# Turning two token blocks through one two-bank PSUM tile, and the tail of the first attention ahead of weight conversions

## The chip, the cores and the metric

The kernel runs on one core of one Trainium2 chip. The metric is the device time of one execution in microseconds (us). Each kernel was run several times beside runs of the kernel before on the same chip; medians are quoted with the lowest and the highest run. All runs and all profiles used here have the state fast. A profile comes from one execution, which need not be the median one. Its span is some 2 us shorter than the device time (531.5 us for 533.2).

## The reference

A gated linear attention for 4 batches, 8 heads, 768 tokens and head size 48, followed by a token mixer of rank 32 and a two-layer channel mixer of 384 to 1536 to 384, all in fp32:

```python
for t in range(S):
    state = f[:, :, t, :, None] * state + np.einsum('bhd,bhe->bhde', k[:, :, t], v[:, :, t])
    y[:, :, t] = np.einsum('bhd,bhde->bhe', q[:, :, t], state)
...
xt = x.transpose(0, 2, 1)
h = xt @ U @ V
u = x + h.transpose(0, 2, 1)
ch = np.maximum(u @ w_ch1, 0.0) @ w_ch2
return (u + ch).astype(np.float32)
```

The weights arrive as 64-bit floats and are converted on the chip.

## The kernel before

A batch is four attention units of two heads each. The attention of batch b is interleaved with the mixer of batch b-1, except for the first batch, which has nothing to be interleaved with. There TensorE has gaps, and the author fills some with dummy products of the identity (`busy`) that are meant to keep its clock up. A unit forms, in this order for TensorE, the turned gates, keys (kz) and queries (qT), the sums that enter the state (ds), and the scores (sc); then its output y in two halves, the read of the state and the product of the masked scores (A) with v. A marker copy on ScalarE (seen) stands between the two halves. One weight is converted by two instructions on ScalarE, three on VectorE and one on GpSimd, through a tile `w_y` of which there are two.

```python
def turn(t):                                   # Mixer; one block of 128 tokens
    a = t // 2
    if t % 2 == 0:
        uT[a] = three.tile([P, NDC, 2 * P], F32, name="uT")
    pt = ps_mm.tile([P, 512], F32, name="put", tag="mm")        # one bank, two such buffers
    for m in range(NDC):
        nc.tensor.transpose(pt[:, m * P : (m + 1) * P], x[:, t, m * P : (m + 1) * P], ident)
    if t % 2:
        busy(pt, 2)                            # dummies into the same bank, first batch only
    o = (t % 2) * P
    nc.scalar.copy(uT[a][:, :, o : o + P], pt[:, 0 : NDC * P].rearrange("p (m t) -> p m t", t=P))
# ... cut
# the first batch: tail of the attention, then the mixer
busy(2)
for piece in loads[: early + 1] + rear(HP - 1, "read") + [lambda: busy(2)] + rear(HP - 1, "inner"):
    piece()                                    # loads[i]: one weight's conversion; early is 3
busy(3)
loads = loads[early + 1 :]
m = mixer(0)
start = m.before[:5] + m.firsts[0:1] + m.before[5:7] + m.firsts[1:2] + m.before[7:9]
for i, (_, piece) in enumerate(start + m.firsts[2:]):
    if loads and (i == 0 or i > 4):
        loads.pop(0)()
    piece()
```

`m.before` holds the low-rank product, the sum over groups, the mix (products and the additions to x), then the turns. `m.firsts` holds the first-layer products (names pz and L201 in the profile), each of 128 x 512 outputs for two blocks. ps_mm has two one-bank buffers; ps_big has three two-bank buffers, used for attention and for the mix.

## Time and profile before

| | before |
|---|---|
| median of the runs quoted with the change | 533.25 us (532.75 to 533.78) |
| span of the profile | 531.5 us |
| TensorE busy | 95% |
| granted clock, mean | 0.977 |

The profile has two records of TensorE (and two weight loads) for one fp32 product, and one for a transpose. The granted clock is TensorE's clock as the profile records it, 1.00 for full and 0.50 for half. A row of the costliest groups gives line, engine, operation, output and inputs with their shapes, count, busy time and mean of one, then the engine's idle time just before and what ended it. A row of the list of waits gives who waited for whom, the total, how often, and the longest. First a row of the page, then two rows of the waits of the kernel before from 44 to 90 us:

```profile
L201 PE MATMUL pz<-uT,w 128*128 128x256 f32 x864 | 196.1, 385 | 4.1 <-ACT uT L193 4.1
```

```profile
ACT h L154 <- PE ph L143: 3.4, 1, 3.4
...
PE pz L201 <- ACT uT L193: 3.7, 3, 1.5
```

The first-layer products waited 4.1 us in all for copies of uT, 3.7 of it in the first batch. The copy of h on ScalarE was released by L143, a dummy, and not by the product that it copies.

### The profile page before, as it was taken

To read this page: it belongs to the slowest core of one execution; us is meant where nothing else is said; L and a number is where in the kernel's file an instruction comes from. 1 tells how busy PE (TensorE), PEld (TensorE's weight loads), DVE (VectorE), ACT (ScalarE), POOL (GpSimd) and SP (SyncE) were. 2 spreads that over 40 slices of the span, in tenths; PEclk is the share of its full clock that TensorE was granted. 3 is DMA by queue.
4 is the path that set the end of the run, shared out by engine and by line. 5 is a ranking of instruction groups with operands and counts; after the bars stand their busy time and mean duration, and the time that the engine had idled before them with its cause. 6 is when DMAs were issued, how large, how long until landed. Compare 5 with 4: busy or idle time off the path is not lost.

```text
span 531.5 us, 12234 instructions
## 1 busy us (share of the span) xinstructions
PE 502.3 (95%) x5405; PEld 422.4 (79%) x5405; DVE 269.5 (51%) x396; ACT 146.8 (28%) x297; POOL 30.1 (6%) x49
## 2 busy tenths in 40 slices
PE   6897879999989889999999999999999999999995
PEld 6786558886677546889889877889889878998995
DVE  5885365554678966665666634544222340222232
ACT  2433265551234223232322303321220122102010
POOL 3001134330000000000000000000000000000000
PEclk9996889999999899999999999999999999999998
DMA  9989905423367842241623500010000000000001
GB/s 148 155 214 187 188 19 172 156 71 81 84 96 113 114 85 38 38 59 19 115 29 62 81 5 29 1 23 31 3 2 30 1 31 1 1 30 1 15 17 35
DMA packets 149269, 34.32 MB, mean 65 GB/s; under 512 B 139798, under 2 KB 147670, under 8 KB 149206
## 3 DMA queue, kind: packets, MB, share of 16 engines
q1 hardware_dynamic: 149206, 33.44, 33.0%
q8 instruction: 44, 0.72, 0.6%
q14 instruction: 19, 0.16, 0.1%
HBM read 28.70 MB, written 4.72 MB: 63 GB/s over the span
## 4 chain that ended last, share of the span: by engine, by line
PE 84%; DVE 7%; ACT 4%; issue 2%; DMA 1%; SPq 1%; POOL 1%; DVEq 0%; ACTq 0%; POOLq 0%
PE pz L201 36%; PE pw L246 24%; PE po L223 6%; PE y L664 3%; PE pt L514 2%; PE y L682 2%; PE sc L597 2%; PE ds L634 2%; PE idle L756 2%; DVE Y L566 2%; PE pt L618 2%; DVE X L548 1%; DVE st L649 1%; PE pu L177 1%; PE put L189 1%
## 5 line engine op out<-in xcount | busy, mean ns | idle before, releaser
L201 PE MATMUL pz<-uT,w 128*128 128x256 f32 x864 | 196.1, 385 | 4.1 <-ACT uT L193 4.1
L201 PEld LDWEIGHTS pz<-uT,w 128*128 128x128 f32 x864 | 162.9, 191 | 28.0 <-ACT uT L193 4.0
L208 ACT ACTIVATE z<-pz 128x512 f32<-128x512 f32 x63 | 37.6, 597 | 144.6 <-PE pz L201 140.5
L246 PE MATMUL pw<-w,z 128*128 128x192 f32 x324 | 56.5, 329 | 0.4 <-DVE o L167 0.4
L246 PE MATMUL pw<-zw,w_raw 128*128 128x192 f32 x324 | 55.9, 327 | 0.0
L246 PEld LDWEIGHTS pw<-w,z 128*128 128x128 f32 x324 | 52.8, 190 | 2.3 <-DVE o L167 1.6
L246 PEld LDWEIGHTS pw<-zw,w_raw 128*128 128x128 f32 x324 | 53.0, 190 | 1.3 <-DVE o L167 1.2
L167 DVE TENSOR_TENSOR w_raw<-z 128x768 f32<-128x768 f32 x18 | 17.2, 955 | 55.3 <-ACT z L208 55.3
L548 DVE TENSOR_TENSOR_SCAN X<-fz,ends 128x768 f32<-128x768 f32 x16 | 28.1, 1757 | 18.2 <-ACT fz L535 15.0
L566 DVE TENSOR_TENSOR_SCAN Y<-fz,starts 128x768 f32<-128x768 f32 x16 | 27.9, 1746 | 0.2
L223 PE MATMUL po<-w,zw 128*128 128x384 f32 x72 | 27.0, 519 | 0.5 <-issue 0.5
L604 DVE TENSOR_TENSOR A<-sc,causal 128x768 f32<-128x768 f32 x16 | 15.2, 950 | 23.1 <-PE sc L597 23.1
L68 POOL TENSOR_TENSOR w<-w_y,w_r 128x384 int32<-128x384 int32 x24 | 24.0, 999 | 46.0 <-DVE w_y L67 46.0
L223 PE MATMUL po<-w,z 128*128 128x384 f32 x72 | 25.1, 493 | 1.2 <-DVE o L167 1.2
L649 DVE TENSOR_TENSOR_SCAN st<-added,whole 128x576 f32<-128x576 f32 x16 | 21.7, 1355 | 6.8 <-ACT added L640 6.7
L167 DVE TENSOR_TENSOR w_y<-x,pw 128x192 f32<-128x192 f32 x9 | 3.2, 355 | 38.9 <-ACT w_y L259 38.9
L622 ACT COPY kb<-pt 128x768 f32<-128x768 f32 x16 | 12.8, 798 | 35.7 <-PE pt L618 35.7
L65 DVE TENSOR_SCALAR w_y<-w_y 128x384 f32<-128x384 f32 (+3 forms) x27 | 9.7, 361 | 25.4 <-ACT w_y L63 25.4
L664 PE MATMUL y<-st,qT 48*64 48x48 f32 x704 | 20.3, 265 | 1.5 <-issue 1.5
L664 PEld LDWEIGHTS y<-st,qT 48*64 48x64 f32 x704 | 17.1, 151 | 5.6 <-issue 4.9
L223 PEld LDWEIGHTS po<-w,zw 128*128 128x128 f32 x72 | 13.5, 198 | 9.7 <-issue 2.8
L223 PEld LDWEIGHTS po<-w,z 128*128 128x128 f32 x72 | 13.0, 190 | 9.5 <-DVE o L167 1.8
(105 smaller groups left out, 529.0 us busy)
## 6 DMA issues: line engine op xcount, KB each, us to landing
w_raw<-in_moe_w_ch_dram SPq DMA_DIRECT2D x18, 384.0 KB, 3.1
out_dram<-o SPq DMA_DIRECT2D x24, 192.0 KB, 2.0
f_raw<-in_f_logit_dram SPq DMA_DIRECT2D x16, 144.0 KB, 3.4
k_raw<-in_k_dram SPq DMA_DIRECT2D x16, 144.0 KB, 4.0
q_raw<-in_q_dram SPq DMA_DIRECT2D x16, 144.0 KB, 4.1
v_nat<-in_v_dram SPq DMA_DIRECT2D x16, 144.0 KB, 4.2
v_nat<-in_v_dram SPq DMA_DIRECT2D x32, 72.0 KB, 3.0
zw<-in_moe_w_ch_dram SPq DMA_DIRECT2D x6, 384.0 KB, 7.2
```

The lines of the kernel that those rows point to most:

```text
L68: nc.gpsimd.tensor_tensor(dst.bitcast(I32), shaped(y.bitcast(I32)), shaped(r), ALU.add)
L167: nc.vector.tensor_tensor(*args)
L201: nc.tensor.matmul(pm[:, i * 2 * P : (i + 1) * 2 * P], lhsT=w1[:, m, o : o + P], rhs=uT[a][:, m, :], start=(m == 0), stop=(m == NDC - 1))
L208: nc.scalar.activation(z[a, c][:, k : k + 2, :].rearrange("p i t -> p (i t)"), pm, AF.Relu)
L223: nc.tensor.matmul(pm, lhsT=z[a, i // NI][:, i % NI, s * P : (s + 1) * P], rhs=w2[:, i, :], start=(i == 0), stop=(i == NFC - 1))
L246: nc.tensor.matmul(pm[:, n * HM : (n + 1) * HM], lhsT=lhs[:, i, :], rhs=rhs[:, i, :], start=(i == 0), stop=(i == NI - 1))
L548: nc.vector.tensor_tensor_scan(backwards(X, S - 1, S), backwards(f, S, S), backwards(ends, S - 1, S), 0.0, ALU.mult, ALU.add,)
L566: nc.vector.tensor_tensor_scan(Y, f[:, 0:S], starts, 0.0, ALU.mult, ALU.add)
L604: nc.vector.tensor_tensor(T["A"], sc[:, :, 0 : NBL * C].rearrange("p h (c i) -> p h c i", i=C), causal.unsqueeze(1).unsqueeze(1).broadcast ...
L622: nc.scalar.copy(kb.rearrange("p h c d -> p h (c d)"), pt[:, :, 0 : NBL * PAD])
L649: nc.vector.tensor_tensor_scan(st, added[:, 0 : D * NCH], T["whole"].rearrange("p e c -> p (e c)"), 0.0, ALU.add, ALU.mult)
L664: nc.tensor.matmul(o(c % 2, par, c // 2), lhsT=T["q"][rows[par], chunk[c]], rhs=T["st"][rows[par], c, :], start=(c <= 2), stop=False, skip ...
```

## The change

Its intent: take TensorE's waits and dummies out of the 40 us between the first attention and the steady first-layer products, and free the turns of all batches from the pace of ScalarE. Two blocks are turned into the two banks of one ps_big tile and copied by one instruction; in the first batch, four blocks are turned ahead of the first product and the last two right after it; the dummies write to a bank of their own; on ScalarE the end of the last attention unit goes ahead of all conversions but two. In the opening, kz (keys) goes ahead of the state scan on VectorE, and two dummies go.

```diff
-        def busy(pm, n):
-            for _ in range(n if wide else 0):
-                nc.tensor.matmul(pm[:, DM : DM + P], lhsT=ident, rhs=ident, start=True, stop=True)
...
-            busy(pm, 2)            # low_rank and added_up: ahead of the copies of h
...
-            if t == NCH - 1:
-                busy(pu[0][:, 1], 3)
...
-        def turn(t):
+        def turn(a):
+            uT[a] = three.tile([P, NDC, 2 * P], F32, name="uT")
+            pt = ps_big.tile([P, 2, 512], F32, name="put", tag="big")
+            for s in range(2):
+                for m in range(NDC):
+                    nc.tensor.transpose(pt[:, s, m * P : (m + 1) * P], x[:, 2 * a + s, m * P : (m + 1) * P], ident)
+            nc.scalar.copy(
+                uT[a].rearrange("p m (s t) -> p s m t", s=2),
+                pt[:, :, 0 : NDC * P].rearrange("p s (m t) -> p s m t", t=P),
+            )
...
-        busy(8)
+        busy(6)
...
-            pieces = front(n, "keep") + rear(n - 1, "scan") + front(n, "keys") + rear(n - 1, "scores")
+            pieces = front(n, "keep", "keys") + rear(n - 1, "scan", "scores")
...
-        busy(2)
-        for piece in loads[: early + 1] + rear(HP - 1, "read") + [lambda: busy(2)] + rear(HP - 1, "inner"):
+        for piece in loads[:2] + rear(HP - 1, "read", "inner") + loads[2 : early + 2]:
             piece()
-        busy(3)
-        loads = loads[early + 1 :]
+        loads = loads[early + 2 :]
...
-        start = m.before[:5] + m.firsts[0:1] + m.before[5:7] + m.firsts[1:2] + m.before[7:9]
-        for i, (_, piece) in enumerate(start + m.firsts[2:]):
-            if loads and (i == 0 or i > 4):
-                loads.pop(0)()
-            piece()
+        start = m.before[:5] + m.firsts[0:1] + m.before[5:]
+        idles = {0: 3, 1: 2, 2: 2}
+        for i, (_, piece) in enumerate(start + m.firsts[1:]):
+            busy(idles.get(i, 0))
+            piece()
+            if loads and i not in (1, 2):
+                loads.pop(0)()
```

## The prediction

> **What bounds the kernel now.** I read the page first: busy shares and the chain that ended last.
>
> ```profile
> PE 502.3 (95%) x5405; PEld 422.4 (79%) x5405; DVE 269.5 (51%) x396; ACT 146.8 (28%) x297; POOL 30.1 (6%) x49
> ...
> PE 84%; DVE 7%; ACT 4%; issue 2%; DMA 1%; SPq 1%; POOL 1%; DVEq 0%; ACTq 0%; POOLq 0%
> ```
>
> TensorE is the bound almost everywhere. From 120 us to the end, the list of waits gives it under 7 us of waiting in 410 us. So the change can gain only where TensorE waits, runs dummy products, or runs slowly. The 40 slices show two dips of its clock (6 and 8 tenths), near 50 and 70 us. I therefore read the chain of waits from 38 to 82 us:
>
> ```profile
> 40.26 1.54 issue
> ...
> 50.49 0.44 ACT w_r L64
> 50.93 0.05 ACT seen L671
> 51.02 1.53 PE y L682 x48
> 52.55 1.58 PE idle L756 x6
> 54.13 2.71 PE ph L150 x12
> 56.84 0.73 PE ph L143 x4
> 57.58 0.49 ACT h L154
> ```
>
> Columns are start, length, and what. The last attention unit's second half (L682) waits for the marker copy "seen" on ScalarE, which stands behind conversions of weights. The copy of h, in turn, waits 0.73 us for dummy products L143. Next, the timeline of 60 to 80 us:
>
> ```profile
> 64.37 2.83 PE L201 MATMUL pz<-uT,w 128*128 128x256 f32 x12 [0.66 <-ACT uT L193]
> ...
> 69.88 0.48 ACT L193 COPY uT<-put 128x384 f32<-128x384 f32 x1
> ...
> 70.41 4.54 PE L201 MATMUL pz<-uT,w 128*128 128x256 f32 x12 [1.53 <-ACT uT L193]
> ...
> 78.15 9.12 PE L201 MATMUL pz<-uT,w 128*128 128x256 f32 x41 [1.52 <-ACT uT L193]
> ```
>
> A first product is 12 records. In the steady stretch they come every 216 ns (162 in 35.13 us, from 84.73), so one product takes 2.59 us. Here the first three take from 64.37 to 78.15 + 2.59 = 80.74: 16.4 us in place of 7.8. Between them TensorE turns two blocks and waits for ScalarE, where the copies of uT stand behind conversions. The second also takes 4.54 us. The busy time and granted clock of each microsecond say why (window, length, busy time of TensorE, its weight loads, VectorE, ScalarE and GpSimd, then granted clock, DMA share, GB/s):
>
> ```profile
> 43.00:44.00 1.00, 0.86 (x36) 0.86 (x39) 0.00 (x0) 0.09 (x1) 0.00 (x0) 0.64 0.79 164
> 44.00:45.00 1.00, 1.00 (x48) 1.00 (x45) 0.00 (x0) 0.35 (x1) 0.00 (x0) 0.50 0.67 120
> ...
> 56.00:57.00 1.00, 1.00 (x5) 0.24 (x2) 0.00 (x0) 0.00 (x0) 0.23 (x1) 0.53 0.93 129
> 57.00:58.00 1.00, 0.55 (x4) 0.35 (x4) 0.00 (x0) 0.42 (x1) 0.00 (x0) 1.00 0.73 200
> ...
> 69.00:70.00 1.00, 0.00 (x0) 0.00 (x0) 0.93 (x4) 1.00 (x4) 0.20 (x1) 1.00 0.00 0
> 70.00:71.00 1.00, 0.59 (x2) 0.51 (x3) 1.00 (x1) 0.53 (x2) 0.80 (x1) 0.80 0.00 0
> 71.00:72.00 1.00, 1.00 (x4) 0.82 (x3) 0.93 (x4) 0.84 (x2) 0.24 (x1) 0.50 0.00 0
> ```
>
> The clock is at half from about 43.3 to 56.9 us and from 70.6 to 74.0 us. Last, the later batches' turns (timeline at 320 us):
>
> ```profile
> 320.78 3.39 PE L189 MATMUL put<-ident,x 128*128 128x128 f32 x18
> ...
> 322.50 0.76 PEld L189 LDWEIGHTS put<-ident,x 128*128 128x128 f32 x6 [0.36 <-ACT uT L193]
> ...
> 324.07 2.86 PE L201 MATMUL pz<-uT,w 128*128 128x256 f32 x12
> ```
>
> TensorE counts as busy here, yet the 18 transposes need 3.29 us, because two one-bank buffers make each pair wait for a copy; six transposes alone take 0.66 us (the chain's rows of put and pt), so 18 could take 1.98.
>
> **What the Trainium skill says.** "TensorE: Matmul & The Clock Gate", Part 1, has the clock at half or full, set by free-running windows of 3413 ns. The trace agrees: 43.3, 56.9, 70.6 and 74.0 lie 4, 4 and 1 such windows apart. The page's closing table asks for no idle gaps over about 3 us; here a window with a gap of 1.54 us (about half busy, with small products) was enough to lose the clock. Its Part 4 says transposes do not count as busy "the same way"; the trace does not bear this out, as the clock stayed 1.00 through 432 to 441 us, over 3 us of it turns. "ScalarE: Activation LUTs", What ACT_TABLE_LOAD costs, has 186 ns + 0.833 ns per element: 506 and 826 ns for 384 and 768. The trace has 478 (uT) and 798 (kb, also PSUM to SBUF), so the measured 0.80 us is used for the new copy. "PSUM — Partial Sum Buffer", PSUM bank collisions, asks for guarding by bank: this agrees with the copy of h starting at 57.58, only after dummies in other columns of its bank.
>
> **The change part by part.**
>
> 1. *Opening.* Two dummies fewer (4 records, 0.87 us at the cold 217 ns) ahead of the first transposes, and kz ahead of the st scan on VectorE (1.36 us earlier for kz, 0.93 later for st). TensorE waited for kz only in unit 1 (until 18.47, though its dummies ended at 17.5). There up to 0.97 us can come forward. VectorE is nearly full in units 0 and 1, and the DMA share of each microsecond stays above 1 until 16 us, so later loads and stalls can absorb it. I take 0.5 us, between 0 and 1.2.
>
> 2. *Tail of attention.* Scores end at 46.34. Now two conversions (U, part of V) and two pairs of dummies lie between this and L682. After the change the order is read (1.5 us at half clock), seen (0.2 with handover), L682 (1.53), all ahead of the other conversions: L682 ends at about 49.6 in place of 52.55. Then three dummies (1.58) as now, to 51.2; the x copy (0.64) is beside them, and U is ready at 48.9. The product L150 starts at 51.2 in place of 54.13: 2.9 us.
>
> 3. *Low rank to the first product.* The dummies move to their own bank, so h is copied at once: -0.73 and about -0.5; the three dummies ahead of the turn (L143 at 61.7, 0.86) go, of which the x addition lets about 0.4 count. Walking it through: L150 51.2 to 53.9, h to 54.4, L159 to 55.3, h to 55.85, L177 from 56.0, first addition 56.95 to 57.85 (0.95 after L177's start, as now), six transposes to 58.75, one copy to 59.55, first product at 59.7. That is 8.5 us in place of 10.24: 1.7. The new copy of two blocks is about as late as the second of two 0.48 us copies, but ScalarE spends 0.80 in place of 0.96.
>
> 4. *First three products.* The second turn now stands before the first product, and its copy (after one conversion) ends at 61.3, before the second product at 63.1. The third turn (0.7 on TensorE) follows the first product; its copy, behind conversions, ends at about 65.0, before 65.7. So the three take 3 x 2.59 + 0.7 = 8.5 us in place of 16.4: 7.9 us, of which 1.7 is clock.
>
> 5. *Later turns.* Each batch turns through three two-bank buffers, free of ScalarE's pace. From the first transpose to the first product: 3.43, 3.29 and 3.95 us now (the last with a small extra transpose), against 2.0, 2.0 and 2.2. Sum: 1.4 + 1.3 + 1.7 = 4.4 us.
>
> Sum: 0.5 + 2.9 + 1.7 + 7.9 + 4.4 = 17.4 us on the bounding engine, and 533.3 - 17.4 = 515.9. Nothing downstream is late enough to eat it: 15 products follow at 2.59 us, while one weight costs ScalarE 1.1 and GpSimd 1.0 us; the raw tiles landed around 61 to 64 us, before their new use at 65.
>
> **The rivals.**
>
> A. *The clock.* The dummies lie differently and fewer are left. Against the gain: half clock from 43 us may last beyond L150, or a window around 57 to 63 us with gaps and transposes may throttle again; each such window costs up to 1.7 us. For it: the stall at 40.26 may fall otherwise in the windows and no throttling happen at all; then scores, reads, dummies and L150 (9 us) run up to 4 us quicker. Result 519 to 521, or 512.
>
> B. *Weights become the wait.* Conversions are bunched before and between the turns, and two w_y buffers allow about one per 1.6 us (starts 67.73, 69.00, 70.83). If copies of uT or h queue behind stalled conversions, TensorE waits as now. My walk has slack of 0.7 us at the third copy, 1.8 at the second. It could cost 1 to 3 us: 517 to 519.
>
> C. *Hidden anyway.* If the wait only moved to the next limit (raw weights or VectorE at 70 to 110 us), parts 2 to 4 would be lost and only the later turns stay: 529. Against it: from 84.73 TensorE runs 162 records without a gap, with VectorE about half busy.
>
> **Range and chances.** Rival A is the widest term, both ways; B adds on one side, and part 1 is uncertain by 0.7. I expect 516, with 512.5 to 520 eight times in ten. The 2% line is at 522.7, which needs C or several losses together: faster 0.93, same 0.06, slower 0.01.
>
> **What would show it.** Right: no ScalarE release ahead of the second and third first-products; steady 216 ns from the first product on; 18 transposes in about 2.0 us in each later batch; L682 starting within 0.4 us of the read's end; the first product about 4.5 to 5.5 us earlier and the fourth about 12.5 to 13 us earlier. Wrong: granted clock 0.5 between 57 and 70 us; long idle on TensorE with releaser uT at 60 to 66 us; a gap ahead of the fourth product for w.

## The result, and the profile after

The changed kernel takes 515.5 us (515.03 to 516.34, 4 runs) against 533.25 us (532.75 to 533.78) on the same chip. The ratio is 0.9669, with a 95% interval of 0.9652 to 0.9686. A ratio is the mean time of one kernel's runs over that of the other's of the same rounds, so it is not quite the ratio of the medians.

The page after, its busy row and its row of first-layer products (L192 is now what L201 was):

```profile
PE 490.7 (96%) x5375; PEld 416.9 (81%) x5375; DVE 272.1 (53%) x396; ACT 144.5 (28%) x285; POOL 31.5 (6%) x49
...
L192 PE MATMUL pz<-uT,w 128*128 128x256 f32 x864 | 193.8, 382 | 0.1
```

The products' wait for uT is gone from the whole program. The timeline after, TensorE's rows around the tail of the attention and the first products (start, length, engine, line, operation, count, and in brackets the idle time before it and its releaser):

```profile
45.12 0.36 PE L588 MATMUL sc<-qT,kz 48*64 48x64 f32 x2 [1.89 <-issue]
...
47.02 1.53 PE L673 MATMUL y<-v_nat,A 64*64 64x48 f32 x48 [0.25 <-ACT seen L662]
...
50.05 2.37 PE L145 MATMUL ph<-x,U 128*32 128x384 f32 x12
...
58.40 2.83 PE L192 MATMUL pz<-uT,w 128*128 128x256 f32 x12
...
61.72 10.53 PE L192 MATMUL pz<-uT,w 128*128 128x256 f32 x48
```

The second half of the last attention unit waits 0.25 us for the marker copy. From 58.40 us on the products follow each other with only the third turn between them. The later turns, timeline after at 306 us:

```profile
306.13 2.13 PE L180 MATMUL put<-ident,x 128*128 128x128 f32 x18
...
308.10 2.75 PE L192 MATMUL pz<-uT,w 128*128 128x256 f32 x12
```

The 18 transposes run without a wait, 1.97 us to the next product. The busy time and clock of each microsecond, after, with the columns that the prediction explains:

```profile
45.00:46.00 1.00, 0.88 (x30) 0.88 (x34) 0.36 (x1) 0.00 (x0) 0.00 (x0) 0.52 1.19 203
...
51.00:52.00 1.00, 1.00 (x8) 0.18 (x2) 0.93 (x3) 0.92 (x2) 0.16 (x1) 0.56 1.30 209
```

The clock is still lost, now from 45.0 to 51.9 us (0.52 and 0.56 are the microseconds in which it changes), after the 1.89 us stop of TensorE in the scores, but there is no second half-clock stretch during the first products. How long the clock is lost differs from run to run of one kernel: the yardstick's profile below, of the same changed kernel, has it at half from 43.0 to 53.3 us. Where the time went, by milestones of the two traces:

| step | before | after | gained | predicted |
|---|---|---|---|---|
| 1. start to the end of the last scores | 46.3 | 45.6 | 0.7 | 0.5 |
| 2. from there to the low-rank product L150 (L145 after) | 54.06 - 46.3 | 50.05 - 45.6 | 3.3 | 2.9 |
| 3. from there to the first first-layer product | 10.31 | 8.35 | 2.0 | 1.7 |
| 4. from there to the fourth (worked out with 2.59 us a product: before, one product after the start of the third; after, two after the start of the second) | 16.37 | 8.50 | 7.9 | 7.9 |
| 5. turns of batches 1, 2, 3 (first transpose to first product) | 3.43, 3.29, 3.95 | 1.96, 1.97, 2.07 | 4.7 | 4.4 |

The sum is 18.6 us; the spans differ by 531.5 - 513.3 = 18.2. Step 1 is not shown by this: in the yardstick's profile the last scores ended at 46.56 us, later than in the kernel before.

### The profile page after: what moved, and what is told of

It reads as the page before. It is cut to its first block, busy times and chain, and to the rows that moved or that the text cites. A ratio compares the mean times of both kernels' runs of the same rounds, so it can differ in the third digit from the quotient of the medians.

```text
span 513.3 us, 12160 instructions
## 1 busy us (share of the span) xinstructions
PE 490.7 (96%) x5375; PEld 416.9 (81%) x5375; DVE 272.1 (53%) x396; ACT 144.5 (28%) x285; POOL 31.5 (6%) x49
## 4 chain that ended last, share of the span: by engine, by line
PE 80%; SPq 8%; DVE 5%; DMA 3%; issue 2%; ACT 1%; DVEq 0%; ACTq 0%
PE pz L192 37%; PE pw L237 24%; PE po L214 5%; SPq L399 4%; SPq L393 3%; PE y L655 3%; PE sc L588 2%; PE ds L625 2%; PE pt L505 2%; DMA f_raw<-in_f_logit_dram 2%; PE put L180 2%; PE y L673 2%; SPq L386 1%; PE pt L609 1%; DMA v_nat<-in_v_dram 1%
## 5 line engine op out<-in xcount | busy, mean ns | idle before, releaser
L192 PE MATMUL pz<-uT,w 128*128 128x256 f32 x864 | 193.8, 382 | 0.1
L192 PEld LDWEIGHTS pz<-uT,w 128*128 128x128 f32 x864 | 161.9, 190 | 22.8 <-issue 0.3
L68 POOL TENSOR_TENSOR w<-w_y,w_r 128x384 int32<-128x384 int32 x24 | 25.3, 1055 | 34.6 <-DVE w_y L67 33.7
L613 ACT COPY kb<-pt 128x768 f32<-128x768 f32 x16 | 12.8, 798 | 31.3 <-PE pt L609 31.3
```

Source lines behind the costliest of these rows:

```text
L68: nc.gpsimd.tensor_tensor(dst.bitcast(I32), shaped(y.bitcast(I32)), shaped(r), ALU.add)
L192: nc.tensor.matmul(pm[:, i * 2 * P : (i + 1) * 2 * P], lhsT=w1[:, m, o : o + P], rhs=uT[a][:, m, :], start=(m == 0), stop=(m == NDC - 1))
```

## The experiments

All are edits of the changed kernel, and all results were correct. They ran in four groups, on three chips, where the kernel before took 531.91 us (529.54 to 534.26), 533.49, 533.03 and 532.1 us. So single runs spread by about 1% there, more than in the first measurement, and differences under 1 us are left to the traces. The yardstick ran on one chip only; its interval and the first measurement of the changed kernel serve for the others.

### The yardstick

No edit.

> The changed kernel as it is, as the yardstick for the runs beside it. Both theories: 515.5 us, 0.967 of the kernel before.

Measured: 515.51 us (514.82 to 516.99, 6 runs), ratio 0.9697 (0.967 to 0.9723). Its profile is of a run of 516.42 us.

### The tail of the attention as before

```diff
-        for piece in loads[:2] + rear(HP - 1, "read", "inner") + loads[2 : early + 2]:
+        busy(2)
+        for piece in loads[: early + 1] + rear(HP - 1, "read") + [lambda: busy(2)] + rear(HP - 1, "inner") + loads[early + 1 : early + 2]:
```

> The changed kernel with the old tail of the first attention (conversions and dummies ahead of the second half of the last unit). Theory: L682's counterpart waits again for the marker copy behind conversions, the first low-rank product starts about 3.3 us later, 518.8 us. Rival (the later steps have slack and absorb it, or the clock comes back earlier relative to the work): under 1.5 us, below 517.0.

Measured: 518.88 us (518.11 to 522.22), 3.4 us over the yardstick of the same chip; ratio 0.978 (0.9741 to 0.9819), which does not overlap the yardstick's. Its timeline:

```profile
50.57 1.53 PE L673 MATMUL y<-v_nat,A 64*64 64x48 f32 x48 [1.77 <-ACT seen L662]
...
53.61 1.89 PE L145 MATMUL ph<-x,U 128*32 128x384 f32 x12
```

The wait for the marker copy is back at 1.77 us, in place of 0.25. From the end of the last scores (45.85 us) the low-rank product starts 7.8 us later, as in the kernel before, against 4.5 in the trace after and 4.6 in the yardstick's. Step 2 of the prediction holds, in mechanism and size. The run puts back the conversions and the two pairs of dummies together, so it does not divide the 3.3 us between them.

### The turns each just ahead of its own product

```diff
-        start = m.before[:5] + m.firsts[0:1] + m.before[5:]
+        start = m.before[:4] + m.firsts[0:1] + m.before[4:5] + m.firsts[1:2] + m.before[5:]
-        for i, (_, piece) in enumerate(start + m.firsts[1:]):
+        for i, (_, piece) in enumerate(start + m.firsts[2:]):
```

> The changed kernel with two-block turns, but the second and third turn again each just ahead of its own product. Theory (the order of turns, not their form, removed the waits in the first batch): TensorE waits for uT twice, about 1.8 us each, 3.5 us slower, 519.0. Rival (one copy in place of two is what counts): under 1 us slower, 516.5 or less. A half-clock window from the gaps would add up to 1.7 us more.

Measured: 519.69 us (519.25 to 521.04), 4.2 us over the yardstick; ratio 0.9779 (0.9745 to 0.9813). Its timeline:

```profile
58.95 2.83 PE L192 MATMUL pz<-uT,w 128*128 128x256 f32 x12 [0.98 <-ACT uT L181]
...
64.02 2.86 PE L192 MATMUL pz<-uT,w 128*128 128x256 f32 x12 [1.59 <-ACT uT L181]
...
69.13 6.09 PE L192 MATMUL pz<-uT,w 128*128 128x256 f32 x27 [1.59 <-ACT uT L181]
```

With the two-block form but the old order, TensorE waits for uT three times, 0.98 + 1.59 + 1.59 us; the first of them lies ahead of the first product, and so in step 3. The fourth product would start at 69.13 + 2.59 = 71.7, so from the first product the stretch is 12.8 us, against 16.4 before and 8.5 after: the order alone is worth 4.3 us of step 4's 7.9. The clock was full in these products (it was back at 51.7 us); the 4.56 us product of before accounts for 2.0 of the remaining 3.6 us. The rest goes with the shorter turn (one copy, no dummies ahead of it), which no run separated further.

### Conversions ahead of the copies

```diff
             busy(idles.get(i, 0))
-            piece()
             if loads and i not in (1, 2):
                 loads.pop(0)()
+            piece()
```

> The changed kernel, but each conversion of a weight is put on ScalarE ahead of the piece that it now follows: ahead of the copy of h, of the copies of uT and of the eviction of each product. Theory (what the change removed are waits of TensorE for copies queued behind conversions): the first h copy comes about 0.5 to 1 us later, the first copy of uT about 1 us, so 1.5 to 2.5 us slower, 517.5, with waits of TensorE for h and uT in the trace. Rival (conversions have slack on ScalarE, which is a quarter busy): under 0.5 us.

Measured: 517.13 us (516.71 to 517.62), ratio 0.9711 (0.967 to 0.9751), against 515.5 for the changed kernel in both of its measurements: 1.6 us. The times alone do not separate it by their intervals; its trace does. The two waits, from its timelines of TensorE and ScalarE:

```profile
54.62 0.91 PE L153 MATMUL ph<-h,blocks 128*128 128x384 f32 x2 [1.61 <-ACT h L148]
```

```profile
53.21 0.56 ACT L63 ACTIVATE w_y<-zw 128x384 f32<-128x384 f32 x1 [0.93 <-POOL w L68]
...
54.10 0.46 ACT L148 COPY h<-ph 128x384 f32<-128x384 f32 x1
```

The copy of h stands behind a conversion that itself waits 0.93 us for GpSimd to free one of the two w_y buffers, and TensorE waits 1.61 us for it. A ScalarE that is a quarter busy still delays the bound engine if its queue is in the wrong order. The waits for uT that were expected too did not appear: the list of waits has 0.3 us for it in this stretch, on a weight load.

### One-block turns in the later batches

```diff
-        parts += [lambda a=a: turn(a) for a in range(NA)]
+        parts += [lambda a=a: turn(a) for a in range(NA)] if wide else [lambda t=t: turn_one(t) for t in range(NCH)]
```

`turn_one` is the old turn without its dummies.

> The changed kernel with one-block turns through the two one-bank buffers in batches 1 to 3 only. Theory: 18 transposes take 3.3 us again in place of 2.0 in each later batch, 4.4 us slower, 519.9. Rival (the time is made up elsewhere, as TensorE counts as busy in either): under 1 us.

Measured: 520.08 us (519.86 to 520.29), ratio 0.9762 (0.9714 to 0.9809): 4.6 us over 515.5. The interval just touches the yardstick's, but its fastest run is 2.9 us above the slowest run of the changed kernel in either measurement. Its timeline for batch 2:

```profile
307.96 3.39 PE L192 MATMUL put<-ident,x 128*128 128x128 f32 x18
```

The next product starts at 311.26, so the stretch is 3.30 us again; those of batches 1 and 3 are back at 3.43 and 3.96. TensorE counts as busy through this stretch in both forms, so the share of busy time could not have shown this gain; the time from the first transpose to the next product does. Step 5 holds. Whether the six banks or the single copy for two blocks carries it, no run separates.

### The dummies of the low-rank stage in their old places

```diff
+            busy(pm, 2)            # in low_rank and in added_up, ahead of the copy of h
-        idles = {0: 3, 1: 2, 2: 2}
+        idles = {0: 3}
```

> The changed kernel with the dummies of the low-rank stage back in the bank of the product, ahead of the copies of h and of the first addition. Theory: copies of h wait for the dummies, 0.7 and 0.5 us, and the addition or the turn 0.4: 1.6 us slower, 517.1. Rival (ScalarE is busy with conversions at that time, so the copies would not start earlier anyway): under 0.5 us.

Measured: 517.03 us (515.75 to 517.1), ratio 0.9698 (0.965 to 0.9746). By the times this is not told from the changed kernel. Its trace has the waits that were expected, 0.57 us ahead of the sum (for the first copy of h) and 0.71 ahead of the mix (for the second):

```profile
54.58 0.91 PE L159 MATMUL ph<-h,blocks 128*128 128x384 f32 x2 [0.57 <-ACT h L154]
...
56.65 1.56 PE L177 MATMUL pu<-h,V 32*128 32x384 f32 x12 [0.71 <-ACT h L162]
```

The stretch from the low-rank product to the first product is 60.47 - 50.93 = 9.54 us, against 8.35 in the trace after and 8.51 in the yardstick's. So the mechanism of step 3 is shown, at about 1.1 us. The edit is smaller than its expectation says: it puts back the dummies ahead of the two copies of h, but not the three ahead of the first addition and the turn, for which the prediction counted 0.4 us and which no run tests. Of step 3's 2.0 us, 0.4 is the low-rank product itself (2.77 us before, 2.37 after), which ran at half clock for less of its length.

### No dummies ahead of and in the low-rank stage

```diff
-        idles = {0: 3, 1: 2, 2: 2}
+        idles = {}
```

> The changed kernel without the seven dummies ahead of and in the low-rank stage. If the clock does not depend on them: TensorE starts the low-rank product 0.6 us earlier, 514.9. If they bring the clock back: full clock comes one window of 3.41 us later, at about 55 us in place of 51.6, and the low-rank stage and its successors run at half clock, 1 to 2 us slower, 517.

Measured: 517.91 us (516.78 to 519.97), ratio 0.9735 (0.9686 to 0.9784): 2.4 us over the yardstick, but the intervals overlap. The clock stayed at 0.50 until 60.2 us in its profile, against 51.9 us in the trace after and the 55 us that were expected:

```profile
60.00:61.00 1.00, 1.00 (x5) 0.85 (x4) 0.93 (x3) 1.00 (x3) 0.00 (x0) 0.88 0.95 292
```

In the other 12 profiles of the changed kernel and its variants it was back by 54.5 us. The stretch from the low-rank product to the first product grew to 59.60 - 48.48 = 11.1 us. So the seven dummies bring the clock back sooner, as far as one profile shows it. That they pay for themselves, by about 2.4 us, is likely but not shown by the times.

### The opening as before

```diff
-        busy(6)
+        busy(8)
-            pieces = front(n, "keep", "keys") + rear(n - 1, "scan", "scores")
+            pieces = front(n, "keep") + rear(n - 1, "scan") + front(n, "keys") + rear(n - 1, "scores")
```

> The changed kernel with the old opening (eight dummies, the st scan ahead of kz). Theory of the prediction (kz earlier brings TensorE forward in unit 1 and this lasts): 0.5 us slower, 516.0. Rival, from the trace after (TensorE stops after the same number of its instructions in both kernels, 1450 and 1706 records of products and weight loads, so it waits there for the next block of its own instructions, and what comes forward ahead of such a stop is lost in it): within 0.3 us of the control, with the stop in the scores of unit 3 shorter than the 1.9 us of the changed kernel and ending within 0.5 us of the same time, 45.1.

Measured: 516.13 us (515.06 to 517.5), ratio 0.9707 (0.9681 to 0.9734), 0.6 us over the yardstick with intervals that overlap. This decides for neither expectation: the rival asked for under 0.3 us, and the stop in the scores did shrink, to 0.33 us, but ended at 45.79, 0.67 us later than 45.12 and not within 0.5. What the traces show is where the time that came forward is lost again. Timelines of the kernel before and of the changed one:

```profile
6.04 0.82 PE L514 MATMUL pt<-ident,f_raw 128*128 128x128 f32 x6
```

```profile
5.47 1.49 PE L505 MATMUL pt<-ident,f_raw 128*128 128x128 f32 x6
...
19.99 0.84 PE L505 MATMUL pt<-ident,f_raw 128*128 128x128 f32 x6 [1.06 <-DMA f_raw<-in_f_logit_dram]
```

With two dummies fewer the first transposes start 0.57 us earlier, but run slowly (1.49 us in place of 0.82), and the first scan starts 0.09 us later (7.89 for 7.80). The earlier kz does bring TensorE forward in unit 1, from 18.47 to 17.54; but before 19.99 it then waits 1.06 us for the gates of unit 2 to arrive. Whatever came forward later was decided by another kind of stop, "issue". Instructions begun since the start, at each stop, for the kernel before and the changed one (window, length, then TensorE products and weight loads with their counts):

```profile
0.00:40.28 40.28, 33.00 (x725) 29.65 (x725) 30.26 (x39) 14.47 (x30) 4.66 (x22) 1.00 1.03 174
```

```profile
0.00:43.25 43.25, 35.90 (x853) 32.11 (x853) 31.89 (x40) 15.87 (x33) 4.67 (x22) 1.00 1.04 183
```

The kernel before stops after 725 + 725 = 1450 records. So does the changed one, at 39.80 us, though the work at that place differs by the removed dummies (the 9th record of the read in place of the 5th); its row shows the next stop, after 853 + 853 = 1706 records, which is 256 more. "Runtime: NRT & Kernel Launch", Instruction fetch mechanics, in the Trainium skill says that an engine's instructions are refilled in blocks of 16 KiB, 256 instructions, with the cost mostly hidden. The page of this profile has 44 packets and 0.72 MB on the instruction queue, 16.4 KB each. The size of a block agrees; "mostly hidden" does not hold here. The trace's DMA records have the landing of these packets too: in all 14 profiles each of the two stops, where it occurs, ended 1.3 to 1.6 us after such a packet had landed (before: landed at 40.40 and 44.27 us, stops over at 41.80 and 45.80; after: 38.86 and 43.78, over at 40.30 and 45.12). So TensorE waits here for its own instructions.

The stop at 1706 ends 4.0 us after the one at 1450 in the kernel before (41.80 to 45.80), 4.8 in the trace after (40.30 to 45.12), 4.0 with the old opening (41.79 to 45.79) and 5.1 with the old order of turns. So a TensorE that reaches the place earlier mostly waits longer there: 0.33 us with the old opening, 1.89 in the trace after. The stop at 1450 is in all 14 profiles. The one at 1706 is in ten; in the yardstick's profile, of the same kernel as the trace after, the stop at 1450 took 1.74 us and the scores then ran through at half clock:

```profile
45.02 1.54 PE L588 MATMUL sc<-qT,kz 48*64 48x64 f32 x48
```

### Loads of the next batch held back

```diff
-            elif n > 1:
-                load(n + 2, "f", "k", "q", "v")
...
+            if data and i >= 8:
+                load(*data.pop(0), hold=True)      # a VectorE write of two elements, then the load
```

> The changed kernel with the loads of units 4 and 5 (needed only from 107 us) held back until the first products, each by a tiny VectorE write to its target that the load must follow. Theory (the stop of 1.9 us in the scores of unit 3 is a block of TensorE's instructions arriving late behind these loads, and the half clock from 45 to 51.6 us follows from that stop): the stop shrinks below 0.3 us, granted clock stays 1.00 from 40 to 60 us, 1.9 + about 2.5 us for the clock: 511 us. Rival (the stop has another cause, such as the scores' operands): the stop stays, 515.5 within 0.5.

Measured: 514.73 us (514.3 to 518.04, 6 runs), ratio 0.9666 (0.9628 to 0.9703): not told from the changed kernel. Its profile is of the slowest of these runs, 518.04 us. In it the stop at 1706 records is gone, as expected; but it is missing from the yardstick's profile too, so this is no sign of the edit. TensorE reached that place only after 47.33 us, for it had stopped 1.19 us at 1450 until 44.76. The clock was at half from 22.3 to 29.1 and from 46.2 to 49.6 us, and with full clock in the low-rank product (1.48 us) TensorE waited for ScalarE instead:

```profile
55.25 0.91 PE L153 MATMUL ph<-h,blocks 128*128 128x384 f32 x2 [1.05 <-ACT h L148]
...
57.33 1.56 PE L170 MATMUL pu<-h,V 32*128 32x384 f32 x12 [0.72 <-ACT h L155]
```

That looks like the prediction's rival B, hidden in the changed kernel behind the half clock; the next runs test it. The expected 4.4 us did not come.

### Earlier conversions, alone and with the loads held back

```diff
-                pieces += rear(n, "states") + rear(n - 1, "read", "inner") + rear(n, "scan", "scores")
+                pieces += rear(n, "states", "scan") + loads[:2] + rear(n - 1, "read", "inner") + rear(n, "scores")
...
-        for piece in loads[:2] + rear(HP - 1, "read", "inner") + loads[2 : early + 2]:
+        for piece in rear(HP - 1, "read", "inner") + loads[2 : early + 1]:
```

> The changed kernel with the conversions of U and of the first part of V moved ahead of the last scores (VectorE is idle there), and that of the second block of the first weights after the first copy of h. With the clock at half through the low-rank product, as in the trace after, these conversions are not what ends last, so nothing moves: 515.5 within 0.5 us. If conversions already bound the low-rank stage: 1 us faster or more.

> The two together: loads of units 4 and 5 held back, and the conversions moved. The run with held loads alone lost its stop in the scores of unit 3 and got full clock in the low-rank product, but then waited 1.05 and 0.72 us for the copies of h behind conversions. Theory (rival B of the prediction takes over when the stop and the half clock go): both waits fall under 0.3 us, 1.5 to 2 us faster than held loads alone, 513. Rival (the waits are of another kind, or the gain depends only on where the clock's windows fall): 514.7 within 0.5.

Measured: alone 515.33 us (514.31 to 516.35), ratio 0.9669 (0.9638 to 0.9701), as expected. Together 514.71 us (512.52 to 516.5), ratio 0.9653 (0.9616 to 0.969): the waits for h are down to none and 0.22 us. That proves little, as the low-rank product ran at half clock here (2.54 us), where the changed kernel does not wait for h either; in the next run, with full clock (1.49 us) and the conversions moved, the waits stay at 0.22 us or less, which does speak for rival B. In the profile of this run the stop at 1706 records is back, 2.16 us, and half clock from 45.9 to 52.7 with it. It ended 5.1 us after the stop at 1450, with the loads of units 4 and 5 out of the way. So those loads do not by themselves cause it. Two of six runs took 512.5, which fits a clock or a stop that fell well, but no run shows which.

### The same without the dummies of units 2 and 3

```diff
-            pieces += [lambda: busy(8)] + rear(n, "kept")
+            pieces += ([lambda: busy(8)] if n < 2 else []) + rear(n, "kept")
```

> As the run with held loads and moved conversions, but without the eight dummies (32 records of products and weight loads) in units 2 and 3. Theory of the blocks (TensorE stops at fixed counts of its own records, 1450 and 1706 in all kernels so far, because the next block comes 4 to 7 us after the one before was entered): the stops stay at 1450 and 1706 records, though that is now about 64 records further on in the work (late in the read of unit 2, and in the read of unit 3), and as the dummies' time (2.0 us each) and a quarter of a block go, it is 1 to 3 us faster, 512 to 513.5. Rival (the dummies hold the clock up): half clock begins in unit 2 or 3 already and it is slower, 516 to 517. If stops belong to the work and not to the count, they stay after the ninth product of the read of unit 2.

Measured: 516.17 us (513.64 to 519.11), ratio 0.9713 (0.9682 to 0.9745): no gain, and a wider spread. Its profile is of the fastest of these runs, 513.64 us. Its timeline:

```profile
37.43 1.16 PE L657 MATMUL y<-st,qT 48*64 48x48 f32 x41
42.45 0.45 PE L657 MATMUL y<-st,qT 48*64 48x48 f32 x3 [3.85 <-issue]
```

The stop moved from after the 9th product record of this read to after the 41st: 32 product records, and as many weight loads, further on, exactly what the 16 dummies had used (two records of each kind per dummy). It grew to 3.85 us and ended at 42.45, later than before, 1.5 us after a packet of the instruction queue had landed; the clock fell to half at 40 us, and the stop at 1706 did not occur. So the stop belongs to the count of instructions and not to the work, and in this profile time saved ahead of it was lost in it. The rival is not excluded: it forecast half clock already in unit 2 or 3 and 516 to 517 us, and both came, though here the clock fell only 1.5 us into the stop.

## Why the prediction was right, and where a step was not

The time, 515.5 for 516.0, and the mechanism of four of the five steps were right.

1. *Opening.* The size (0.5 for 0.7 in one trace) is not shown to be right: in two profiles of the changed kernel the last scores end at 45.60 and 46.56 us, further apart than the gain. The step's "two dummies fewer" gained nothing: the transposes after them ran slowly. Its kz gain of up to 0.97 us occurred as 0.93 and was eaten within 2.5 us by the wait for f_raw, which the step had named as a risk. What remains at the end of the scores depends on the stops at 1450 and 1706 records, which the step did not have; the run with the old opening leaves 0.6 us, which its interval does not tell from nothing. That the size fits is luck as far as the runs show.
2. *Tail.* Right: 3.3 us in the trace for 2.9, and 3.4 when undone. The read took less after the scores than the 1.5 us assumed, as it began while the scores' last records ran.
3. *Low rank.* Right: 2.0 for 1.7; the copies' wait for dummies in their bank is shown by the run with the old places, at 1.1 us. Of the rest, 0.4 us is the clock, which the step did not count on.
4. *First products.* Right: 7.9 for 7.9. The order of the turns carries 4.3 us of it, by the run that undoes it; the 2.0 us of clock and the shorter turn are read from the traces alone. The walk's copies came earlier than worked out (the third ended 63.45 for 65.0), and nothing waited.
5. *Later turns.* Right: 4.7 for 4.4, and 4.6 when undone.

In the times, the runs that undo steps 2 to 5 in part give back 3.4 + 1.5 + 4.2 + 4.6 = 13.7 us of the 17.75 gained. Of the signs that the prediction named, the first product came 6.0 us earlier (4.5 to 5.5 forecast) and the fourth 13.8 (12.5 to 13); the other signs of being right appeared, and none of being wrong.

Of the rivals, A (the clock) was not avoided, but it was milder: half clock from 45.0 to 51.9 us in place of 43.3 to 56.9. This is in part luck of the run: its length up to 62 us is 6.8 and 10.2 us in the two profiles of the changed kernel, and 3.4 to 13.7 in those of the variants, with 13.7 not only in the run without dummies but also in the one with conversions moved. B needs a wrong order in ScalarE's queue; that costs 1.6 us, as the run with conversions ahead shows. C fell: what was undone of steps 2 and 4 came back in full in the time.

What stays open: why a block of instructions lands so late in this stretch, and what would bring it sooner. Holding the unit loads back did not settle it; the loads of the first weights, which still ran then, were not tried.

## What to carry to other kernels

Where one engine is the bound, look at the stretches where its neighbours' queues decide its order: a copy that it waits for should stand ahead of work that nobody waits for yet, even on an engine that is a quarter busy. A stream of small transposes needs enough PSUM buffers, or few enough copies, to run ahead of them, and the share of busy time does not show when it lacks them; time the stretch instead. Dummy products can be worth their time for the clock, but in a bank that no copy waits for, and they also use up instructions, which a stretch of very short products can run out of. And when one profile shows a stop or a slow clock, look at a second profile of the same kernel before reading a difference from it.

## What the Trainium skill lacked or had wrong

- "Runtime: NRT & Kernel Launch", Instruction fetch mechanics: crossing a block of 256 instructions is called mostly hidden. Here TensorE stopped for 0.3 to 3.9 us after 1450 and 1706 of its products and weight loads, with products of 64 x 48 at about 88 records per us; from one of these stops to the next took 3.7 to 5.4 us in the profiles, and each ended 1.3 to 1.6 us after a packet of the instruction queue had landed. The page does not say how fast blocks can follow each other.
- "TensorE: Matmul & The Clock Gate", closing table of rules: gaps to avoid are put at over about 3 us. In the kernel before, one window of 3.41 us with a gap of 1.54 us and small products otherwise, about half busy (1.60 us between 39.87 and 43.28), lost the full clock.
- The same page, Part 4: transposes are said not to count as busy in the same way. In the run without dummies, the window from 56.83 to 60.24 us held 12 transposes for 2.8 us and 0.6 us of a first-layer product, and the full clock came back at its end. What the prediction gives against the page, 1.00 through the turns at 432 to 441 us, is weaker, as turns of 3.95 us need not fill a window.
- No page read here says how much activity of small products counts for the clock: 46.7 to 50.1 us of the kernel before was all but fully busy, nearly half of it with 48 x 48 reads, and the clock stayed at 0.50; a window full of dummies and the low-rank product brought it back at 56.9.
